# The last projection result in two column halves, and one store for four batches

## Chip, core and metric

The kernel runs on one NeuronCore of one Trainium2 chip. The metric is device time in microseconds (us) of one execution of the whole program; the time given is the median of three runs.

## What is computed

Attention over 8 batches and 8 heads with 32 global and 512 local tokens of 64 dimensions per head, followed by a gated projection. Everything is float32. Cut to what matters:

```
# attention: global queries see all 544 keys; local queries see the 32 global keys
# and local keys within a distance of 32
out_g = softmax(q_g k_all^T / 8) v_all            # (8, 8, 32, 64)
out_l = softmax([q_l k_g^T | masked q_l k_l^T] / 8) v_all   # (8, 8, 512, 64)
x = concat(out_g, out_l) over tokens, heads side by side    # (8, 544, 512)

# gate: causal depthwise convolution of 5 taps along the 544 tokens, then a sigmoid
gate = sigmoid(sum_k conv_w[k] * x shifted by 4 - k)
out  = (gate * (x @ w_val)) @ w_out               # (8, 544, 512)
```

## The kernel before

The attention is done unit by unit (32 units: 8 batches by 4 pairs of heads), the projection by function `moe` once per batch for its 512 local tokens (keys 0 to 7), and at the very end once more, with key `"g"`, for the 256 global tokens of all eight batches together. Products keep float32 accuracy by splitting each operand into a high and a low part and running three matmuls for each pair of 128 x 128 weights: high x high, high x low, low x high.

Inside `moe` there are three steps. `g1(e, t)` multiplies by `w_val` and leaves block `e` of the value (128 channels by `n` tokens) in a PSUM bank. `gv`, `gh`, `gl` multiply by the gate and split the product into the tiles `gh` and `gl`. `g2(r, e)` multiplies by `w_out`: for a block `r` of 128 tokens it accumulates, over the four `e`, twelve matmuls of 128 x 512 into one bank. `ob(r)` copies the bank to an SBUF tile (`ob` for batches, `obg` for the global tokens) and `store` writes it out. For the global tokens there are two blocks, `r` = 0 and 1, each of 128 rows: four batches by 32 tokens. In the output those rows are not contiguous, as each batch has 544 rows; `store_g` writes one batch's 32 rows at a time, alternating between the DMA queues of SyncE (SP) and ScalarE (ACT).

The order of all work is written out by hand in the table `ORDER`: each engine carries out its tasks in that order, and the numbers behind `@` name PSUM banks. The class `Plan` replays the table and keeps, in `plan.at`, which bank each result has. The table ends with the global tokens:

```
g1.g.3.3 st.6.3 g2.g.0.0@4 gv.g.3 gh.g.3:DVE g2.g.0.1 ob.7.3 g2.g.0.2 gl.g.3 g2.g.0.3
g2.g.1.0@5 st.7.3 g2.g.1.1 ob.g.0 g2.g.1.2 st.g.0 g2.g.1.3 ob.g.1 st.g.1
```

`g2.g.0.*` is block 0 in bank 4, `g2.g.1.*` block 1 in bank 5, `ob.g.*` the copies and `st.g.*` the stores. The copy of block 1 is shared by two engines: ACT copies columns 0 to 255 and VectorE (DVE) columns 256 to 511 of the same bank into the same tile. After `st.g.1` nothing is left but the wait for the stores and the end of the program. Banks of the `g1.g` results (5, 1, 4, 1) are free again by then. The two tiles of tag `gv` hold the gated products until they are split.

Of the kernel before, what the change touches and what calls it, by code (L numbers as in the profile page):

```python
# [8 lines left out]
F32 = mybir.dt.float32  # L9
# [8 lines left out]
B, H, SL, SG, D = 8, 8, 512, 32, 64  # L18
DM = H * D
KW = 5  # L20
P = 128
NDT = DM // P
# [295 lines left out]
def attention_moe(ctx, tc, qk, vw, maskd, w_val, convT, w_out, out):  # L318
    nc = tc.nc
    V, A, G, T = nc.vector, nc.scalar, nc.gpsimd, nc.tensor  # L320

    cp = ctx.enter_context(tc.tile_pool(name="cp", bufs=1))
    sb = ctx.enter_context(tc.tile_pool(name="sb", bufs=2))
    ps = ctx.enter_context(tc.tile_pool(name="ps", bufs=1, space=PSUM))

    plan = Plan()
    psum = ps.tile([P, 8, SL], F32, name="psum")

    def bank(key):
        return psum[:, plan.at[key][0], :]  # L330
# [23 lines left out]
    wvh, wvl, woh, wol = (cp.tile([P, NDT, DM], F32R, name=n) for n in ("wvh", "wvl", "woh", "wol"))  # L354
# [46 lines left out]
    def copy(name, out, in_):  # L401
        eng = plan.tasks[name].eng
        if eng == "ACT":
            A.copy(out, in_)  # L404
        else:
            (V if eng == "DVE" else G).tensor_copy(out, in_)
# [3 lines left out]
    def on_pe(ins):  # L410
        last_pe[:] = [ins.ins]
# [295 lines left out]
    def moe(key, n, x0, deps_x, deps_gate, before, store):  # L707

        box = {}
        last = before  # L710

        def g1(e, t):
            xh, xl = xs_h[x0 + t], xs_l[x0 + t]
            if t == 0:
                box["pv", e] = bank(f"g1.{key}.{e}")[:, :n]
            for q, (w, x) in enumerate(((wvh, xh), (wvh, xl), (wvl, xh))):
                on_pe(T.matmul(box["pv", e], w[:, e, t * P:t * P + P], x, start=(t == 0 and q == 0),  # L717
                         stop=(t == NDT - 1 and q == 2)))

        def gv(e):  # L720
            if e == 0:
                box["gh"] = sb.tile([P, NDT, n], F32R, tag="gh", name=f"gh{key}", bufs=1)
                box["gl"] = sb.tile([P, NDT, n], F32R, tag="gl", name=f"gl{key}", bufs=1)
            box["gv", e] = sb.tile([P, n], F32, tag="gv", name=f"gv{key}_{e}")
            V.tensor_tensor(out=box["gv", e], in0=box["pv", e], in1=gates[x0 + e], op=ALU.mult)

        def gh(e):
            copy(f"gh.{key}.{e}", box["gh"][:, e, :], box["gv", e])

        def gl(e):  # L730
            V.tensor_tensor(out=box["gl"][:, e, :], in0=box["gv", e], in1=box["gh"][:, e, :].bitcast(F32),
                            op=ALU.subtract)

        def g2(r, e):
            if e == 0:
                box["po", r] = bank(f"g2.{key}.{r}")
            rs = slice(r * P, r * P + P)
            for q, (g, w) in enumerate(((box["gh"], woh), (box["gh"], wol), (box["gl"], woh))):
                on_pe(T.matmul(box["po", r], g[:, e, rs], w[:, e, :], start=(e == 0 and q == 0),  # L739
                         stop=(e == NDT - 1 and q == 2)))  # L740

        def ob(r):
            box["ob", r] = sb.tile([P, DM], F32, tag="ob", name=f"ob{key}_{r}")
            if (key, r) == ("g", n // P - 1):
                A.copy(box["ob", r][:, :DM // 2], box["po", r][:, :DM // 2])
                V.tensor_copy(box["ob", r][:, DM // 2:], box["po", r][:, DM // 2:])
            else:
                copy(f"ob.{key}.{r}", box["ob", r], box["po", r])

        part = 693 if n == 512 else 356  # L750
        early = [f"pc{u}.{KW - 1}" for u in range(NPC)] if key == 0 else []
        for e in range(NDT):
            for t in range(NDT):
                name = f"g1.{key}.{e}.{t}"
                plan.add(name, "PE", part, lambda e=e, t=t: g1(e, t), [last, f"w{e}"] + deps_x(t) + early,
                         take=[("bank", name[:-2])] if t == 0 else [],
                         give=[("xh", x0 + t), ("xl", x0 + t)] if e == NDT - 1 else [])
                last = name
            plan.add(f"gv.{key}.{e}", "DVE", 601 if n == 512 else 334, lambda e=e: gv(e),
                     [last] + deps_gate(e) + ([f"gv.{key}.{e - 1}"] if e else []),  # L760
                     take=[("gv", f"{key}.{e}")] + ([("g", key)] if e == 0 else []),
                     give=[("bank", f"g1.{key}.{e}"), ("gate", x0 + e)])
            plan.add(f"gh.{key}.{e}", (("ACT", 520 if n == 512 else 385), ("DVE", 335 if n == 512 else 205)), 0, lambda e=e: gh(e),
                     [f"gv.{key}.{e}"], lock=True)
            plan.add(f"gl.{key}.{e}", "DVE", 600 if n == 512 else 338, lambda e=e: gl(e), [f"gh.{key}.{e}"], 
                     give=[("gv", f"{key}.{e}")], lock=True)
        for r in range(n // P):
            for e in range(NDT):
                name = f"g2.{key}.{r}.{e}"
                plan.add(name, "PE", 682, lambda r=r, e=e: g2(r, e),  # L770
                         [last, f"gl.{key}.{e}", f"w{NDT + e}"], take=[("bank", name[:-2])] if e == 0 else [],
                         give=[("g", key)] if (r, e) == (n // P - 1, NDT - 1) else [])
                last = name
            plan.add(f"ob.{key}.{r}", *(("ACT", 350) if (key, r) == ("g", n // P - 1) else ((("ACT", 470), ("DVE", 600)), 0)), lambda r=r: ob(r), [last], take=[("ob", name[3:-2])],
                     give=[("bank", name[:-2])])
            plan.add(f"st.{key}.{r}", "ACT", 800 if key == "g" else 400, lambda r=r: store(r, box["ob", r]), [f"ob.{key}.{r}"])
            plan.add(f"sd.{key}.{r}", "DMA", 620, lambda: None, [f"st.{key}.{r}"], give=[("ob", f"{key}.{r}")])
        return last
# [60 lines left out]
    for b in range(B):  # L839
# [4 lines left out]
        for h in range(2):  # L844
            n = f"{b}.{h}"
# [65 lines left out]
    for b in range(B):  # L911
        units = range(4 * b, 4 * b + 4)
        for u in units:
            plan.add(f"sig{u}", "ACT", 530, lambda u=u: sigmoid(gates[u]),
                     [f"fix{v}" if v < NHF else f"conv{v}.{KW - 2}" for v in units] + ([f"sig{u - 1}"] if u % 4 else []))
        last = moe(b, SL, 4 * b, lambda t, b=b: [f"xl{4 * b + t}"], lambda e, b=b: [f"sig{4 * b + e}"], last,
                   lambda r, o, b=b: A.dma_start(out[b, SG + r * P:SG + r * P + P, :], o))
# [16 lines left out]
    plan.add("sigg", "ACT", 1250, lambda: [sigmoid(gates[NU + dt]) for dt in range(NDT)],  # L934
             [f"gconv{dt}" for dt in range(NDT)])

    def store_g(r, o):
        for s in range(P // SG):
            (A if s % 2 else nc.sync).dma_start(out[r * (P // SG) + s, 0:SG, :], o[s * SG:s * SG + SG, :])

    moe("g", B * SG, NU, lambda t: [f"gxl{t}"], lambda e: ["sigg"], last, store_g)

    with tc.manual_schedule():
# [91 lines left out]
```

## Time and profile before

| what | value |
|---|---|
| runs | 362.12 us median of 3 (360.65 to 363.55) |
| profiled execution | 361.64 us |
| its span, first to last instruction | 359.9 us |
| mean granted TensorE clock | 0.994 of full speed |
| busy share of the span: TensorE, its weight loads, VectorE, ScalarE | 97%, 78%, 88%, 71% |
| DMA | 66.73 MB, mean 185 GB/s; 8.91 MB written |
| last matmul starts | 355.33 us |

PE is TensorE's matmul row and PEld its weight loads; an issue of a DMA is listed on the queue of the engine that issues it (SPq, ACTq), and what it moves is seen apart, as packets and as the landing. Times in the trace count from the start of the span.

### The profile page before, as it was taken

To read this page: it belongs to the slowest core of one execution; us is meant where nothing else is said; L and a number is where in the kernel's file an instruction comes from. 1 tells how busy PE (TensorE), PEld (TensorE's weight loads), DVE (VectorE), ACT (ScalarE), POOL (GpSimd) and SP (SyncE) were. 2 spreads that over 40 slices of the span, in tenths; PEclk is the share of its full clock that TensorE was granted. 3 is DMA by queue.
4 is the path that set the end of the run, shared out by engine and by line. 5 is a ranking of instruction groups with operands and counts; after the bars stand their busy time and mean duration, and the time that the engine had idled before them with its cause. 6 is when DMAs were issued, how large, how long until landed. Compare 5 with 4: busy or idle time off the path is not lost.

```text
span 359.9 us, 14810 instructions
## 1 busy us (share of the span) xinstructions
PE 349.9 (97%) x6331; PEld 280.0 (78%) x6331; DVE 315.3 (88%) x1085; ACT 254.3 (71%) x652; POOL 0.8 (0%) x7
## 2 busy tenths in 40 slices
PE   8899999899999999999999999999999999999995
PEld 4666687778787888788878877888878888888894
DVE  4899999999989899899899997989599696988981
ACT  3899999897897688987788566776659458523131
POOL 0000000000000000000000000000000000000000
PEclk9899999999999999999999999999999999999999
DMA  7995947695675734925666482823854101000223
GB/s 280 400 362 166 359 156 279 209 402 193 226 235 199 276 104 108 391 102 171 221 241 237 159 277 104 262 67 132 283 165 173 62 2 51 13 29 36 112 87 87
DMA packets 17249, 66.73 MB, mean 185 GB/s; under 512 B 1952, under 2 KB 4000, under 8 KB 17184
## 3 DMA queue, kind: packets, MB, share of 16 engines
q1 hardware_dynamic: 12240, 57.12, 45.2%
q10 hardware_dynamic: 4944, 8.67, 6.6%
q8 instruction: 49, 0.80, 0.9%
q14 instruction: 16, 0.13, 0.1%
HBM read 56.87 MB, written 8.91 MB: 183 GB/s over the span
## 4 chain that ended last, share of the span: by engine, by line
PE 81%; ACT 8%; DMA 5%; DVE 3%; issue 1%; SPq 1%; ACTq 0%; DVEq 0%
PE psum L717 25%; PE psum L739 23%; PE psum L603 7%; PE psum L567 7%; PE psum L592 7%; PE psum L632 4%; DMA v<-in_vw_dram 3%; PE psum L531 3%; DMA out_dram<-ob 2%; ACT pm L586 2%; PE psum L493 2%; ACT xs L624 2%; PE psum L511 1%; DVE gate L668 1%; ACT xc L404 1%
## 5 line engine op out<-in xcount | busy, mean ns | idle before, releaser
L586 ACT ACTIVATE pm<-pm,mx 128x128 f32<-128x128 f32 x256 | 80.9, 407 | 25.8 <-DVE mx L579 22.5
L668 DVE SCALAR_TENSOR_TENSOR gate<-xc,cw,gate 128x512 f32<-128x512 f32 x120 | 87.7, 745 | 1.1 <-ACT gate L397 0.4
L579 DVE CUSTOM_DVE_ANT_0 pm<-psum,mask 128x128 f32<-128x128 f32 x256 | 57.4, 285 | 5.2 <-PE psum L567 5.2
L717 PE MATMUL psum<-xh,wvh 128*128 128x512 f32 x128 | 53.8, 421 | 0.0
L739 PE MATMUL psum<-woh,gh 128*128 128x512 f32 x128 | 53.0, 414 | 0.0
L717 PE MATMUL psum<-xl,wvh 128*128 128x512 f32 x128 | 50.6, 396 | 0.0
L717 PE MATMUL psum<-xh,wvl 128*128 128x512 f32 x128 | 50.5, 395 | 0.0
L739 PE MATMUL psum<-woh,gl 128*128 128x512 f32 x128 | 50.2, 392 | 0.0
L739 PE MATMUL psum<-wol,gh 128*128 128x512 f32 x128 | 50.0, 391 | 0.0
L404 ACT COPY pts<-psum 128x512 f32<-128x512 f32 x49 | 28.6, 601 | 16.0 <-PE psum L592 16.0
L592 PE MATMUL psum<-ident,pm 128*128 128x128 f32 x256 | 38.0, 278 | 0.6 <-ACT pm L586 0.3
L567 PE MATMUL psum<-qk 64*32 64x128 f32 x2048 | 38.1, 281 | 0.5 <-ACT pm L586 0.4
L603 PEld LDWEIGHTS psum<-v,pts 128*32 128x32 f32 x2048 | 31.1, 111 | 8.3 <-issue 4.7
L567 PEld LDWEIGHTS psum<-qk 64*32 64x32 f32 x2048 | 30.3, 108 | 8.5 <-issue 3.6
L592 PEld LDWEIGHTS psum<-ident,pm 128*128 128x128 f32 x256 | 29.6, 140 | 9.1 <-ACT pm L586 2.7
L603 PE MATMUL psum<-v,pts 128*32 128x65 f32 x2048 | 34.9, 224 | 1.4 <-DMA v<-in_vw_dram 1.2
L717 PEld LDWEIGHTS psum<-xh,wvl 128*128 128x128 f32 x128 | 24.0, 188 | 5.6 <-issue 0.2
L739 PEld LDWEIGHTS psum<-woh,gl 128*128 128x128 f32 x128 | 24.0, 188 | 5.3
L717 PEld LDWEIGHTS psum<-xh,wvh 128*128 128x128 f32 x128 | 24.3, 190 | 4.5 <-DVE xl L664 0.2
L717 PEld LDWEIGHTS psum<-xl,wvh 128*128 128x128 f32 x128 | 24.2, 189 | 4.1 <-issue 0.2
L739 PEld LDWEIGHTS psum<-woh,gh 128*128 128x128 f32 x128 | 24.2, 189 | 4.0 <-issue 0.2
L739 PEld LDWEIGHTS psum<-wol,gh 128*128 128x128 f32 x128 | 24.2, 189 | 3.9
(111 smaller groups left out, 554.0 us busy)
## 6 DMA issues: line engine op xcount, KB each, us to landing
v<-in_vw_dram SPq DMA_DIRECT2D x32, 975.0 KB, 6.7
qk<-in_qk_dram SPq DMA_DIRECT2D x32, 624.0 KB, 5.0
out_dram<-ob ACTq DMA_DIRECT2D x32, 256.0 KB, 2.2
wraw<-in_w_val_dram SPq DMA_DIRECT2D x4, 512.0 KB, 12.3
wraw<-in_w_out_dram SPq DMA_DIRECT2D x4, 512.0 KB, 4.1
mask<-in_mask_dram SPq DMA_DIRECT2D x1, 256.0 KB, 4.6
out_dram<-obg SPq DMA_DIRECT2D x4, 64.0 KB, 1.7
out_dram<-obg ACTq DMA_DIRECT2D x4, 64.0 KB, 2.0
```

Source lines behind the costliest of these rows:

```text
L404: A.copy(out, in_)
L493: on_pe(T.matmul(s[h][SG * c:SG * c + SG, cols], qkt[rows, SL + SG * h:SL + SG * h + SG], keys, start=True, stop=True))
L531: on_pe(T.matmul(ag[SG * c:SG * c + SG, :], pgt[:k, s, SG * c:SG * c + SG], vt[:k, w, h, :], start=(n == 0), stop=(n == len(steps) - 1)))
L567: on_pe(T.matmul((sx, sy)[h][32 * j:32 * j + 32, i, :], qkt[rows, 32 * m:32 * m + 32], qkt[rows, k0:k0 + P], start=True, stop=True))
L579: V.tensor_tensor_reduce(out=pm[:, h, i, :], in0=s[:, i, :], in1=mask[:, i, :], op0=ALU.add, op1=ALU.min, scale=-SCALE, scalar=3.0e38, acc ...
L586: A.activation(out=pm[:, h, i, :], in_=pm[:, h, i, :], func=AF.Exp, bias=mx[:, c:c + 1], scale=-1.0)
L592: on_pe(T.transpose(pt[:, i, :], pm[:, h, i, :], ident))
L603: on_pe(T.matmul(ax[32 * j:32 * j + 32, h, E1 * i:E1 * i + E1], pts[:, h, i, 32 * j:32 * j + 32], vt[:, block_win(4 * i + j), h, :], start ...
L632: on_pe(T.transpose(xt[:, P * i:P * i + P], xs[:, i].rearrange("p h d -> p (h d)"), ident))
L668: V.scalar_tensor_tensor(out=acc, in0=xc[:, k:k + SL], scalar=cw[:, u % NDT, k:k + 1], in1=acc, op0=ALU.mult, op1=ALU.add)
L717: on_pe(T.matmul(box["pv", e], w[:, e, t * P:t * P + P], x, start=(t == 0 and q == 0), stop=(t == NDT - 1 and q == 2)))
L739: on_pe(T.matmul(box["po", r], g[:, e, rs], w[:, e, :], start=(e == 0 and q == 0), stop=(e == NDT - 1 and q == 2)))
```

## The change

For block 1 of the global tokens, `g2` no longer runs twelve matmuls of 512 columns. `g2_halves` first runs twelve of 256 columns for output columns 0 to 255 into bank 5 (that of `g2.g.1`), then twelve for columns 256 to 511 into another bank, that of the first `g1.g` result which neither block uses (bank 1). As soon as the first twelve are recorded, VectorE's copy of that half into a tile of its own (`obg_first`, tag `gv`) and its store on the SP queue are recorded too. `ob` copies the second half on ACT into a tile of half the width, and its store follows on the SP queue. `store_g` now writes all four batches of a block with one DMA, whose DRAM side is 4 batches by 32 rows by the columns: block 0 on the ACT queue, both halves of block 1 on the SP queue.

```diff
+        def g2_halves(r, e):
+            if e % (NDT // 2) == 0:
+                used = [plan.at[f"g2.{key}.{i}"][0] for i in (r - 1, r)]
+                spare = next(n for n in (f"g1.{key}.{i}" for i in range(NDT)) if plan.at[n][0] not in used)
+                box["half", e * 2 // NDT] = bank(spare if e else f"g2.{key}.{r}")
+            c, rs = e * 2 // NDT, slice(r * P, r * P + P)
+            for k in range(e * 2 % NDT, e * 2 % NDT + 2):
+                for q, (g, w) in enumerate(((box["gh"], woh), (box["gh"], wol), (box["gl"], woh))):
+                    on_pe(T.matmul(box["half", c][:, :DM // 2], g[:, k, rs], w[:, k, c * DM // 2:(c + 1) * DM // 2],
+                             start=(k == 0 and q == 0), stop=(k == NDT - 1 and q == 2)))
+            if (c, k) == (0, NDT - 1):
+                o = sb.tile([P, DM // 2], F32, tag="gv", name="obg_first")
+                V.tensor_copy(o, box["half", 0][:, :DM // 2])
+                store(r, o, 0)
+
         def g2(r, e):
+            if (key, r) == ("g", n // P - 1):
+                g2_halves(r, e)
+                return
...
         def ob(r):
-            box["ob", r] = sb.tile([P, DM], F32, tag="ob", name=f"ob{key}_{r}")
-            if (key, r) == ("g", n // P - 1):
-                A.copy(box["ob", r][:, :DM // 2], box["po", r][:, :DM // 2])
-                V.tensor_copy(box["ob", r][:, DM // 2:], box["po", r][:, DM // 2:])
+            last_part = (key, r) == ("g", n // P - 1)
+            o = box["ob", r] = sb.tile([P, DM // 2 if last_part else DM], F32, tag="ob", name=f"ob{key}_{r}")
+            if last_part:
+                A.copy(o, box["half", 1][:, :DM // 2])
             else:
-                copy(f"ob.{key}.{r}", box["ob", r], box["po", r])
+                copy(f"ob.{key}.{r}", o, box["po", r])
...
-    def store_g(r, o):
-        for s in range(P // SG):
-            (A if s % 2 else nc.sync).dma_start(out[r * (P // SG) + s, 0:SG, :], o[s * SG:s * SG + SG, :])
+    def store_g(r, o, c=1):
+        k = P // SG
+        cols = slice(0, DM) if r == 0 else slice(c * DM // 2, (c + 1) * DM // 2)
+        (nc.sync if r else A).dma_start(out[r * k:r * k + k, 0:SG, cols], o)
```

On the ACT queue, at the end of the program, the copies of batch results (`ob`) and their stores stay as they were, and the two blocks of global tokens (`obg`) follow. Before:

```order
L404 COPY ob_3_5936<-psum 128x512 [waits DMAHW7_49,PE_49]
L917 DMA out_dram<-ob_3_5936 128x512 [waits Activation_49]
L404 COPY obg_5952<-psum 128x512 [waits DMAHW0_49,PE_49]
L939 DMA out_dram<-obg_5952 32x512 [waits Activation_49]
L939 DMA out_dram<-obg_5952 32x512
L745 COPY obg_5964<-psum 128x256 [waits DMAHW1_49,PE_49]
L939 DMA out_dram<-obg_5964 32x512 [waits DVE_49]
L939 DMA out_dram<-obg_5964 32x512
```

And with the change:

```order
L404 COPY ob_3_5936<-psum 128x512 [waits DMAHW7_49,PE_49]
L935 DMA out_dram<-ob_3_5936 128x512 [waits Activation_49]
L404 COPY obg_5961<-psum 128x512 [waits DMAHW0_49,PE_49]
L958 DMA out_dram<-obg_5961 4x32x512 [waits Activation_49]
L764 COPY obg_5976<-psum 128x256 [waits DMAHW1_49,PE_49]
```

Two stores of block 0 have become one with three counts, and behind the last copy ACT issues nothing.

On the SP queue, which up to there issues the loads of the attention (`v`, `qk`), the end differs like this:

```order
 L416 DMA v_4954<-in_vw_dram 128x1950
 L416 DMA v_5000<-in_vw_dram 128x1950
-L939 DMA out_dram<-obg_5952 32x512 x2
-L939 DMA out_dram<-obg_5964 32x512 x2
-L1030 UNCONDITIONAL_BRANCH
+L958 DMA out_dram<-obg_first 4x32x256
+L958 DMA out_dram<-obg_5976 4x32x256
+L1049 UNCONDITIONAL_BRANCH
```

The four stores of one batch each, two for either block, have become two stores of four batches, one for either half of block 1.

## The prediction

> **What bounds the kernel now.** I read the page's head and its chain first, then the chain of work that ended last from 340 us on.
>
> ```profile
> span 359.9 us, 14810 instructions
> ...
> PE 349.9 (97%) x6331; PEld 280.0 (78%) x6331; DVE 315.3 (88%) x1085; ACT 254.3 (71%) x652; POOL 0.8 (0%) x7
> ...
> PE 81%; ACT 8%; DMA 5%; DVE 3%; issue 1%; SPq 1%; ACTq 0%; DVEq 0%
> ```
>
> ```profile
> 350.27 5.46 PE psum L739 x24
> 355.73 0.02 issue
> 355.75 0.38 ACT obg L745
> 356.13 0.02 issue
> 356.16 0.42 DVE obg L746
> ```
>
> The kernel is a TensorE kernel, 97% busy and 81% of the chain. The change touches nothing before the last 24 matmuls, so the stage that decides is the tail. There the chain is serial: the matmuls end, ACT copies the left half of the last result (0.38 us), VectorE copies the right half only after ACT (its row starts when ACT's has ended: both read one bank and write one tile), and then four stores go out. From the last copy's end at 356.58 to the end of the span at 359.9 are 3.3 us, 1% of the span, in which no compute engine works. That is nearly all the change can win, and the stores are all it can lose on.
>
> How the stores run today is seen in ACT's timeline, in the answers for the two lines that store, in SyncE's waits, and in the DMA picture of the last 3.5 us.
>
> ```profile
> 353.04 0.59 ACT L404 COPY obg<-psum 128x512 f32<-128x512 f32 x1 [2.77 <-PE psum L739]
> 353.65 0.86 ACTq L939 DMA_DIRECT2D out_dram<-obg  x2
> 355.75 0.37 ACT L745 COPY obg<-psum 128x256 f32<-128x256 f32 x1 [2.13 <-PE psum L739]
> 356.62 0.85 ACTq L939 DMA_DIRECT2D out_dram<-obg  x2
> ```
>
> ```profile
> L939 SPq DMA_DIRECT2D out_dram<-obg x4: 315/384/414, 353.6 to 357.0; - x4
> L939 ACTq DMA_DIRECT2D out_dram<-obg x4: 375/412/445, 353.7 to 357.0; - x4
> ...
> DMA to landing us min/median/max: 1.6/1.9/2.0
> ```
>
> ```profile
> L917 ACTq DMA_DIRECT2D out_dram<-ob x32: 338/338/444, 78.2 to 350.3; - x32
> ...
> DMA to landing us min/median/max: 2.0/2.2/8.2
> ```
>
> ```profile
> SPq L1030 <- DMA out_dram<-obg: 1.4, 2, 1.2
> ```
>
> ```profile
> DMA  0000000000769299949999410000000000000000
> ...
> DMA packets 192, 0.26 MB, mean 75 GB/s; under 512 B 64, under 2 KB 64, under 8 KB 192
> ```
>
> Each queue issues two stores of 64 KB, the second at 357.0, and it lands up to 2.0 us later, at 359.0; SyncE waits for it (1.2 us) and closes the program 0.9 us after that. The DMA picture covers 356.5 to 360 in 40 slices of 0.0875 us. It goes quiet after slice 24, at 358.6, so from the last packet to the span's end are 1.3 us. Of the 192 packets 64 are under 512 B, and 128 are rows of 2 KB: four stores, 16 small closing packets each. So a store of 32 rows is now cut over all 16 engines, two rows to an engine.
>
> **The change part by part.**
>
> *The matmuls.* Rows of matmuls of both widths, first and last of their runs:
>
> ```profile
> 344.42 0.28 PE L717 MATMUL psum<-xgh,wvh 128*128 128x256 f32 x1
> ...
> 349.99 0.28 PE L717 MATMUL psum<-xgh,wvl 128*128 128x256 f32 x1
> ...
> 352.83 0.39 PE L739 MATMUL psum<-woh,ghg 128*128 128x512 f32 x1
> ...
> 355.33 0.39 PE L739 MATMUL psum<-woh,glg 128*128 128x512 f32 x1
> ```
>
> The 48 matmuls of 256 columns start 5.57 / 47 = 0.1185 us apart, the last 12 of 512 columns 2.50 / 11 = 0.227 us. The change turns those 12 into 24 of 256 columns. The last one then starts at 352.83 + 23 x 0.1185 = 355.56 and ends 0.28 later, at 355.84, where today's ends at 355.72: +0.12 us. The weights are loaded 24 times in place of 12; the 256-column run pays the same load per matmul and keeps its 0.1185, so that is in the price.
>
> *The copies.* The left half is complete after 12 matmuls, at 352.83 + 11 x 0.1185 + 0.28 = 354.41. VectorE copies it (0.42 us, beside the second half's matmuls in another bank), to 354.86. Behind that copy nothing is queued on VectorE; today it idles there. The right half is copied by ACT from 355.87 to 356.24. The 0.42 us copy leaves the path: the last store can be issued at 356.28, where today the first two go out at 356.62 and the last two at 357.0. Up to here the change gains 0.34 us on the first issue and 0.74 us on the last.
>
> *The stores.* Eight issues become three: one of 256 KB on ACT at 353.65 (row block 0), and on SyncE one of 128 KB at 354.90 (left half) and one of 128 KB at 356.28 (right half). Behind them stands only SyncE's closing wait. Issue time: today's rows of this line are 0.32 to 0.45 us, and the trace has no issue of a store whose DRAM side has three counts (4 batches, 32 rows, columns). The longest single issue nearby in kind is one load's
>
> ```profile
> 2.60 0.86 SPq L416 DMA_DIRECT2D qk<-in_qk_dram  x1
> ```
>
> so the new form costs between 0 and 0.5 us more. I take 0, the nearest row (same queue, same destination), and keep 0.5 for the range.
>
> *How many engines carry a store* is the term that decides, and no row shows it. Every transfer of the trace has an outermost count of 32 or 128 and spreads over 16 engines; the new ones have 4 on the DRAM side. If the rows are still dealt out to 16 engines, an engine gets 8 of them; if the outermost count is what is dealt out, four engines get one batch of 32 rows each and the other twelve nothing. The four stores of before were each one batch: 16 engines were reached because a batch was cut by its 32 rows. I take the second: in the rows so far the cut is along the outermost count and never along an inner one. The Trainium skill has this as a rule ("DMA: Bandwidth & Descriptors", section "Why a DMA increments its semaphore by 16 and not by 1"): a copy runs on the largest number of engines up to 16 that divides the slowest count, other than 1, of both sides, which for 128 partitions and 4 batches is 4; by it the sum is the four-engine one below, without it the 16-engine one. The 16 closing packets per 32-row store agree with it, and no run here shows a count under 16.
>
> Prices for four engines, from three DMA pictures (345 to 352.5 us, 0 to 20 us, 353.5 to 356.6 us):
>
> ```profile
> DMA packets 576, 1.05 MB, mean 140 GB/s; under 512 B 64, under 2 KB 64, under 8 KB 576
> ...
> q10 hardware_dynamic: 576, 1.05, 37.6%
> ```
>
> ```profile
> DMA packets 2788, 6.93 MB, mean 347 GB/s; under 512 B 303, under 2 KB 1825, under 8 KB 2786
> ...
> q1 hardware_dynamic: 2642, 6.88, 91.0%
> ```
>
> ```profile
> DMA  0000000000000979597938989923000000000000
> ```
>
> In the first, 512 rows of 2 KB took 0.376 x 16 x 7.5 = 45.1 us of engine time: 0.088 us a row, 23.3 KB per us and engine. In the second more than half of the packets are of 1 KB (1825 less 303), and the rate is 6.88 MB / (0.91 x 16 x 20) = 23.6 KB per us: the price goes by bytes, so a row of 1 KB takes 0.044 us, with 0.088 as the far end. The third (slices of 0.0775 us) starts at 354.51: data follows the issue at 353.65 by 0.86 us.
>
> On four engines, each has to move 32 x 2 KB and twice 32 x 1 KB: 32 x 0.088 + 64 x 0.044 = 5.63 us, one store behind the other on the same four. The 256 KB store begins at 354.51 and would be done at 357.3; the left half is there from 354.90 + 0.86 = 355.8 and the right half from 357.1, so the engines never run dry, and it no longer matters when the copies end. The last packet ends at 354.51 + 5.63 = 360.14, where today's ends at 358.6: **+1.5 us**. The 1.3 us behind it stay. The copies' gain of 0.74 us and the matmuls' 0.12 us vanish in the wait for these engines.
>
> **The sum.** The profiled execution took 361.64 us, 1.7 us around its span of 359.9; 361.64 + 1.5 = **363.2 us**. (It lies 0.5 us under the median of the three runs, 362.12, and the runs span 360.65 to 363.55, so the forecast is a slight loss that a measurement of this kernel can hardly tell: about 1%, 3.6 us, is what it tells.)
>
> **The rivals.**
>
> - *Sixteen engines.* Then the 256 KB store is gone long before the others start, and the right half is one store alone, issued at 356.28. Its 128 KB lie between the 64 KB that landed in 1.6 and the 256 KB that land in 2.0 us: 1.8, landing at 358.1 against 359.0 today. With 0.5 us more for the issue the gain falls to 0.4. I take 0.9: 360.7 us. For it: DMAs are cut somewhere by rows, and the SBUF side still has 128. Against it: no row with an inner cut. This is the other side, and it decides if more than about six engines share the stores (5.63 x 4/6 = 3.75, ending at 358.3, no later than today's 358.6).
> - *Rows of 1 KB cost as much as rows of 2 KB* on four engines, and the issue is slow: 64 x 0.044 + 0.5 = 3.3 us more, 366.5 us, slower by over 1%. It needs a 1 KB row above 0.076 us; the byte rate of the 0 to 20 us picture speaks against it.
> - *The one store is issued as four again.* Four issues of 0.38 us on SyncE, the last at 357.42, landing 1.6 to 2.0 us later at 359.2 on the mean: 0.2 us later than today, 361.8 us. The three single instructions in each queue's order speak against it.
>
> **How the numbers follow.** Four engines 0.60; sixteen 0.28; taken apart 0.06; dear small rows 0.06. Single runs of before lie up to 1.5 us from their median; I take 1.2 us of scatter for a median of three. The likeliest's own range is then 362.0 to 364.9 (with the slow issue's 0.5 above). For 8 in 10 the range must also reach to the sixteen-engine case, 360.7, and take in a part of its scatter: 360.2 to 364.9. Over 1% either way needs 3.6 us: faster only by scatter on the sixteen-engine case, 0.02; slower with the dear rows or scatter on the forecast, 0.05; within it 0.93.
>
> **What would show it.** In the profile after: 24 rows of about 0.28 us and 0.1185 us apart at the new matmul line, the last ending near 355.8; VectorE's copy near 354.4 with no wait for ACT; one ACT copy as the last compute near 355.9; a SyncE issue near 356.3. With four engines the DMA picture from 354.5 on stands at two to three tenths without a gap until about 360, the three stores bring 12 small packets in place of 48, and landings of the last two stores take 3 us and more. With sixteen, short bursts near full, quiet by 357.6. The forecast is wrong if the plateau is absent, or if the span's end no longer hangs on these stores.

## The result, and the profile after

| | before | after |
|---|---|---|
| median (lowest to highest) | 361.81 us (360.65 to 363.55), 6 runs | 366.59 us (364.34 to 367.24), 6 runs |
| ratio | | 1.0109, 95% interval 1.0076 to 1.0141 |
| profiled execution, its span | 361.64, 359.9 us | 367.24, 365.3 us |

The change makes the kernel slower by about 1.1% (2.7 to 5.1 us by the interval). The forecast was 363.2 us with a range up to 364.9: the right sign, and too small.

The end of the chain of waits of the kernel after (start, length, what):

```profile
351.93 2.73 PE psum L757 x12
354.65 2.88 PE psum L742 x24
357.54 0.02 issue
357.56 0.37 ACT obg L764
```

Beside the chain of before: row block 0 of the global tokens began at 350.27 and begins at 351.93 now, and one copy stands behind the matmuls where there were two. From that point the span went on for 359.9 - 350.27 = 9.6 us, and now goes on for 365.3 - 351.93 = 13.4 us. So the tail, the only part that was changed, is longer by 3.7 us. (These pieces of the chain begin 0.16 us after block 0's first matmul does, which is at 350.11 and 351.77.) The other 1.7 us of the two spans' difference of 5.4 arose earlier, where both kernels do the same. One place is seen in TensorE's waits from 221 to 227 us, first after, then before (what waited for what, us, times, longest):

```profile
PE psum L632 <- ACT ob L404: 2.2, 1, 2.2
```

```profile
PE psum L632 <- ACT ob L404: 0.5, 1, 0.5
```

In the traces of kernels with the same work ahead of it, here and in the experiments below, block 0's first matmul starts anywhere between 350.1 and 353.4 us (the latest is e11). I take these 1.7 us for scatter, and count every tail below from that first matmul, in each kernel's own trace. The ratio agrees with that: its 1.09% is 3.9 us, about what the tail alone makes.

The tail by engine, after. ACT's timeline, VectorE's and SyncE's queue:

```profile
354.69 0.59 ACT L404 COPY obg<-psum 128x512 f32<-128x512 f32 x1 [2.77 <-PE psum L757]
355.31 1.14 ACTq L958 DMA_DIRECT2D out_dram<-obg  x1
357.56 0.37 ACT L764 COPY obg<-psum 128x256 f32<-128x256 f32 x1 [2.28 <-PE psum L742]
```

```profile
356.13 0.42 DVE L746 COPY obg_first<-psum 128x256 f32<-128x256 f32 x1 [2.95 <-PE psum L742]
```

```profile
356.58 0.69 SPq L958 DMA_DIRECT2D out_dram<-obg_first  x1
357.96 0.54 SPq L958 DMA_DIRECT2D out_dram<-obg  x1
```

All compute is done at 357.93, and the program ends 7.4 us later; before, these were 3.3 us. SyncE's waits at the end, and the DMA picture of 354 to 366 us (40 slices of 0.3 us):

```profile
SPq L1049 <- DMA out_dram<-obg_first: 4.5, 1, 4.5
SPq L1049 <- DMA out_dram<-obg: 1.3, 1, 1.3
```

```profile
DMA  2000000004150021222222222222222110000000
...
DMA packets 397, 0.54 MB, mean 45 GB/s; under 512 B 12, under 2 KB 268, under 8 KB 396
```

All rows here are those of the three new stores: the last batch store had ended by 353.7, and the 2 of slice 0 is one packet of instructions. The first row of block 0 moves at 356.6, 1.3 us after its issue, and slices 9 to 11 (counted from 0) hold 12 of its first rows. The picture books the whole time of a row in the slice in which the row starts; these rows take long, so the slices show a 4 and a 5, and those behind them nothing while the rows are still under way. From slice 15 on the stores run at two tenths of 16 engines, with 12 packets under 512 B: four closing packets for each store, where each store had 16 before. Four engines carry them, twelve are idle. Four stretches of the same picture (three of 1 us, one of 2 us):

356.6 to 357.6 us, the first rows of the 256 KB store:

```profile
DMA  2500930300039990009000000000000009900900
...
DMA packets 15, 0.03 MB, mean 31 GB/s; under 512 B 0, under 2 KB 0, under 8 KB 15
```

357.6 to 358.6 us, the next rows of that store:

```profile
DMA packets 14, 0.03 MB, mean 29 GB/s; under 512 B 0, under 2 KB 0, under 8 KB 14
```

359.3 to 360.3 us, later rows of the same store:

```profile
DMA packets 45, 0.09 MB, mean 92 GB/s; under 512 B 0, under 2 KB 0, under 8 KB 45
...
q10 hardware_dynamic: 45, 0.09, 25.4%
```

361.5 to 363.5 us, rows of 1 KB of the two halves:

```profile
DMA packets 186, 0.18 MB, mean 92 GB/s; under 512 B 6, under 2 KB 186, under 8 KB 186
```

In the steady part the four engines are full (25.4% of 16 engines is 4.06 engines): a row of 2 KB takes 4 / 45 = 0.089 us of one engine, and a row of 1 KB 2 x 4 / 180 = 0.044 us (186 packets less 6 closing ones). In the first two microseconds they move 15 and 14 rows in place of 45 each. Single rows of the first have records of up to 0.96 us.

### The profile page after: what moved, and what is told of

Same layout as the page of the kernel before. It is cut to its first block, busy times and chain, and to the rows that moved or that the text cites. A ratio compares the mean times of both kernels' runs of the same rounds, so it can differ in the third digit from the quotient of the medians.

```text
span 365.3 us, 14827 instructions
## 1 busy us (share of the span) xinstructions
PE 348.3 (95%) x6343; PEld 279.4 (76%) x6343; DVE 315.3 (86%) x1085; ACT 254.5 (70%) x652; POOL 0.9 (0%) x7
## 3 DMA queue, kind: packets, MB, share of 16 engines
HBM read 56.87 MB, written 8.91 MB: 180 GB/s over the span
## 4 chain that ended last, share of the span: by engine, by line
PE 83%; ACT 9%; DMA 3%; DVE 1%; issue 1%; ACTq 0%; DVEq 0%
PE psum L717 25%; PE psum L757 23%; PE psum L603 8%; PE psum L567 7%; PE psum L592 7%; PE psum L632 4%; ACT pm L586 3%; DMA out_dram<-ob 3%; PE psum L531 3%; PE psum L493 2%; PE psum L511 2%; ACT xs L624 1%; PE psum L821 1%; ACT pts L404 1%; PE psum L742 1%
## 5 line engine op out<-in xcount | busy, mean ns | idle before, releaser
L567 PE MATMUL psum<-qk 64*32 64x128 f32 x2048 | 36.8, 273 | 1.6 <-issue 0.7
L567 PEld LDWEIGHTS psum<-qk 64*32 64x32 f32 x2048 | 29.2, 106 | 9.5 <-issue 4.2
L603 PE MATMUL psum<-v,pts 128*32 128x65 f32 x2048 | 34.1, 221 | 1.7 <-ACT diag L682 1.6
L725 DVE TENSOR_TENSOR gv<-psum,gate 128x512 f32<-128x512 f32 x32 | 21.9, 686 | 7.3 <-PE psum L717 6.8
```

The costliest lines, as they stand in the source:

```text
L567: on_pe(T.matmul((sx, sy)[h][32 * j:32 * j + 32, i, :], qkt[rows, 32 * m:32 * m + 32], qkt[rows, k0:k0 + P], start=True, stop=True))
L603: on_pe(T.matmul(ax[32 * j:32 * j + 32, h, E1 * i:E1 * i + E1], pts[:, h, i, 32 * j:32 * j + 32], vt[:, block_win(4 * i + j), h, :], start ...
```

## The experiments

The theory from these views: **the stores alone** make the loss, because four engines carry them and because these start slowly; the halves work and are not seen. Rivals: the halves cost something (24 weight loads, the other copy order); any store with three counts is slow whatever its engines; rows of 1 KB are dear; ACT's queue is a bad place for the 256 KB store.

All tails in one table, in us after the first matmul of block 0, read from each trace's instruction and packet records. The ratio is to the kernel before on the same chip; that of e7 rests on two runs. In every row the difference of the tails, as a share of the kernel, lies within the ratio's interval.

| kernel | engines | closing packets | last copy ends | last packet | span ends | ratio (95%) |
|---|---|---|---|---|---|---|
| before | 16 | 128 | 6.47 | 8.53 | 9.75 | |
| after | 4 | 12 | 6.16 | 12.23 | 13.58 | 1.0109 (1.0076 to 1.0141) |
| e1 halves, old stores | 16 | 192 | 7.70 | 9.55 | 10.96 | 1.0048 (1.0026 to 1.0071) |
| e2 new stores, no halves | 4 | 8 | 6.47 | 12.46 | 13.86 | 1.0116 (1.0081 to 1.0151) |
| e3 after, 16 engines | 16 | 48 | 6.16 | 7.91 | 9.29 | 0.9999 (0.9972 to 1.0026) |
| e4 after, block 0 old | 16, halves 4 | 72 | 6.16 | 9.60 | 10.76 | 1.0023 (0.9997 to 1.0049) |
| e5 before, block 0 new on ACT | 4, block 1 16 | 68 | 6.47 | 9.84 | 11.29 | 1.0058 (1.0016 to 1.0099) |
| e6 after, 8 engines | 8 | 24 | 6.16 | 8.78 | 10.13 | 1.0014 (0.9985 to 1.0043) |
| e7 after, 2 engines | 2 | 12 (six stores) | 6.16 | 17.52 | 18.68 | 1.0255 (1.0190 to 1.0319) |
| e8 halves, old stores reordered | 16 | 192 | 6.16 | 8.36 | 9.67 | 0.9997 (0.9967 to 1.0028) |
| e9 16 engines, no halves | 16 | 32 | 6.47 | 8.63 | 10.05 | 0.9993 (0.9962 to 1.0023) |
| e10 as e5, on SP | 4, block 1 16 | 68 | 6.47 | 9.86 | 11.31 | 1.0019 (0.9982 to 1.0057) |
| e11 before, last batch store on 4 | 16, that store 4 | 136 | 6.84 | 8.91 | 10.20 | 0.9994 (0.9962 to 1.0026) |

### One part without the other

**e1**, the halves with stores of one batch each (edit against after):

```diff
-        (nc.sync if r else A).dma_start(out[r * k:r * k + k, 0:SG, cols], o)
+        for s in range(k):
+            (A if s % 2 else nc.sync).dma_start(out[r * k + s, 0:SG, cols], o[s * SG:s * SG + SG, :])
```

> The column halves of the change, but every store covers one batch as before: 32 rows of 2 KB for block 0 and 32 rows of 1 KB for either half, alternating between the two queues (12 stores, each over 16 engines). Theory A (the loss is all in the stores that cover four batches): the copies' gain is seen, the last issue lies at about 0.7 us after the last copy's end less 0.4, the last landing some 0.5 us earlier than before, so 0.3 to 0.9 us faster than before (about 361.2 us). Theory B (the halves themselves cost: 12 more matmuls and their code, or a copy that is late): slower than before by 1 us or more, 363 us and up.

Measured: 363.85 us, 1.0048 (1.0026 to 1.0071), slower than before, though on 16 engines; the tail ends 1.2 us later than before. The cause is a fault of the experiment, seen in ACT's timeline:

```profile
355.81 0.85 ACTq L959 DMA_DIRECT2D out_dram<-obg_first  x2
356.76 0.59 ACT L404 COPY obg<-psum 128x512 f32<-128x512 f32 x1 [5.62 <-PE psum L742]
357.38 0.85 ACTq L959 DMA_DIRECT2D out_dram<-obg  x2
358.33 0.37 ACT L764 COPY obg<-psum 128x256 f32<-128x256 f32 x1 [0.97 <-ACT obg L404]
```

The stores of the left half stand in ACT's order ahead of the copy of block 0. They wait for VectorE's copy, and ACT waits with them: the copy of block 0, which came 2.92 us after block 0's first matmul in the kernel after, came at 5.77 here, and the last copy ended at 7.70 in place of 6.16. So e1 says nothing on the halves; e8 has the stores in another order.

**e2**, the stores without the halves (edit against before):

```diff
-        for s in range(P // SG):
-            (A if s % 2 else nc.sync).dma_start(out[r * (P // SG) + s, 0:SG, :], o[s * SG:s * SG + SG, :])
+        k = P // SG
+        (nc.sync if r else A).dma_start(out[r * k:r * k + k, 0:SG, :], o)
```

> The four-batch stores alone: block 1 is made and copied as before (12 matmuls, ACT then VectorE), each block is written with one store of 4 batches x 32 rows x 2 KB. Theory A: four engines carry 128 KB each, the tail is as long as in the changed kernel, about 3.8 us longer than before from block 0's copy to the end: about 365.5 us. Theory B: close to before, within 1 us of 361.8.

Measured: 365.63 us, 1.0116 (1.0081 to 1.0151), the same loss as after, with matmuls, copies and tiles of before. All rows are 2 KB here, so dear small rows are out, and so are the halves as a cause. Its DMA picture, 354.1 to 366 us:

```profile
DMA  0002413022222222223122222111000000000000
...
DMA packets 264, 0.52 MB, mean 44 GB/s; under 512 B 8, under 2 KB 8, under 8 KB 264
```

Two stores, eight closing packets, two tenths: four engines again, and a thin start.

**e8**, the halves with old stores in an order in which no store waits ahead of a copy (edit against after):

```diff
-        (nc.sync if r else A).dma_start(out[r * k:r * k + k, 0:SG, cols], o)
+        for s in range(k):
+            eng = A if r == 0 or (c == 1 and s % 2) else nc.sync
+            eng.dma_start(out[r * k + s, 0:SG, cols], o[s * SG:s * SG + SG, :])
```

> The halves with stores of one batch again, now with the four stores of the left half all on SyncE's queue and those of block 0 all on ACT's, so that no copy of ACT stands behind a store that waits for VectorE (in the first try with one-batch stores block 0's copy came 2.8 us late for that reason). Theory A: the last copy ends 0.3 us earlier than before, the end of the program 0.3 to 0.5 us earlier in the tail, total 361.5 us, not to be told from before. Theory B (the halves cost by themselves): tail longer than before's 9.75 us, total above 363 us.

Measured: 362.75 us, 0.9997 (0.9967 to 1.0028). The last copy ends 0.31 us earlier than before and the span 0.08 us: twelve issues have taken most of it back. The halves do no harm, and what they gain is too small to be measured.

**e4**, only block 0 as before, the halves in the new form (edit against after):

```diff
+        if r == 0:
+            for s in range(k):
+                (A if s % 2 else nc.sync).dma_start(out[s, 0:SG, :], o[s * SG:s * SG + SG, :])
+        else:
+            nc.sync.dma_start(out[r * k:r * k + k, 0:SG, c * DM // 2:(c + 1) * DM // 2], o)
```

> The changed kernel with block 0 stored batch by batch as before; only the two half stores cover four batches. Four engines then carry 64 KB each (2.7 us) in place of 128 KB. If the slow first rows of 1.5 us came with the 256 KB store on ACT's queue and are gone: the right half's store alone decides, issued at 356.3 on before's clock, last packet near 358.6: no change, 361.5 to 362. If each first store of this form pays them: last packet near 360.1, about 363.3 us.

Measured: 363.09 us, 1.0023 (0.9997 to 1.0049). The tail ends 1.0 us later than before and 2.8 us earlier than after. In SyncE's order the left half's store stands ahead of two of block 0's stores and holds them up, so this is an upper bound for what the halves' stores cost alone. Without block 0's store in the new form 2.8 of the 3.8 us are gone; that store alone makes 1.5 (e5, below). The two parts cost more together than each by itself: in the kernel after, the halves' rows come behind block 0's on the same four engines.

The left half's store also shows a start of its own, on engines that were idle: its first row moves at 357.4, 1.3 us after the issue, and 61 rows of 1 KB follow in the first microsecond, where 90 is the steady number. No record of them is above 0.21 us.

### The number of engines

**e3** and **e9**. The rows of the global tokens are laid out token by token instead of batch by batch (`gv` writes its columns in that order, so the partition is token x 4 + batch), and the DRAM side of a store becomes 32 tokens by 4 batches by columns: the same three counts, bytes and row lengths, with 32 outermost. e3 has the halves, e9 has block 1 as before.

```diff
-            V.tensor_tensor(out=box["gv", e], in0=box["pv", e], in1=gates[x0 + e], op=ALU.mult)
+            if key == "g":
+                o = box["gv", e].rearrange("p (r q b) -> p r b q", r=2, q=SG)
+                i0, i1 = (x.rearrange("p (r b q) -> p r b q", r=2, q=SG) for x in (box["pv", e], gates[x0 + e]))
+                V.tensor_tensor(out=o, in0=i0, in1=i1, op=ALU.mult)
...
-        (nc.sync if r else A).dma_start(out[r * k:r * k + k, 0:SG, cols], o)
+        (nc.sync if r else A).dma_start(out[r * k:r * k + k, 0:SG, cols].rearrange("b q c -> q b c"), o)
```

> The changed kernel, still with three stores of three counts, but with the tokens of a block ordered token by batch (the gated product is written in that order), so that the DRAM side of a store is 32 tokens x 4 batches x columns, its outermost count 32 in place of 4. Theory A1 (the number of engines follows the outermost count): 48 closing packets in place of 12, the DMA picture in short bursts near full, last packet before 359 in the time of before's span: about 361.0 us, as e1 or a little better. Theory A2 (a store with three counts is itself slow, in its issue of 0.5 to 1.1 us and its first rows of 0.2 to 0.9 us, whatever the engines): 16 engines but 1 to 2 us of slow first rows, 362.5 to 364 us. If the cut still goes by batches: as the changed kernel, 366 us.

Measured: 361.94 us, 0.9999 (0.9972 to 1.0026): the loss is gone. The picture of 352 to 360 us (slices of 0.2 us), and the microsecond from 353.0, in which its 256 KB store begins (0.025 us):

```profile
DMA  0000079970049500019800000000000000000000
...
DMA packets 432, 0.52 MB, mean 66 GB/s; under 512 B 48, under 2 KB 304, under 8 KB 432
```

```profile
DMA  0492796898699289689948948994852200000000
...
DMA packets 144, 0.26 MB, mean 262 GB/s; under 512 B 16, under 2 KB 16, under 8 KB 144
```

Three bursts near full, 3 x 16 closing packets. All 128 rows of block 0 are through in 0.8 us, with no slow start, where after moved 15 rows in its first microsecond. So a store with three counts is not slow by itself. Its issue is longer than that of a one-batch store, though; the rows of the storing line in e3 (duration ns min/median/max, start us):

```profile
L963 ACTq DMA_DIRECT2D out_dram<-obg x1: 667/667/667, 351.7 to 351.7; - x1
L963 SPq DMA_DIRECT2D out_dram<-obg_first x1: 652/652/652, 353.0 to 353.0; - x1
L963 SPq DMA_DIRECT2D out_dram<-obg x1: 539/539/539, 354.4 to 354.4; - x1
```

The tail ends at 9.29 against before's 9.75. That is the gain which the change had to give, 0.46 us or 0.13% of the kernel, under what the ratio's interval (0.3% either way) can show; what the other order of `gv`'s writes costs ahead of the tail is in the ratio and not separated.

> Block 1 made and copied as before (12 matmuls of 512 columns, ACT then VectorE), stores of four batches on sixteen engines by the token-by-batch order: two stores in place of eight. Theory A: the store form is neutral once it has sixteen engines; the tail is 9.6 us, between before's 9.75 and the 9.3 of the version with halves and sixteen engines; total 361.8 us. Theory B (most of that version's gain is from the stores): 9.3 us or less.

Measured: 362.14 us, 0.9993 (0.9962 to 1.0023). Two stores in place of eight on 16 engines, and the tail ends 0.3 us later than before: fewer stores gain nothing here.

**e6**, eight engines: a block is 16 tokens of all eight batches, so that the outermost count is 8 (edit against after, with `gv` laid out to match, as in e3).

```diff
-        (nc.sync if r else A).dma_start(out[r * k:r * k + k, 0:SG, cols], o)
+        (nc.sync if r else A).dma_start(out[:, r * (SG // 2):(r + 1) * (SG // 2), cols], o)
```

> The changed kernel with the tokens of the global part dealt to the two blocks differently: a block holds 16 tokens of all eight batches, so the DRAM side of a store is 8 batches x 16 tokens x columns, outermost count 8. If the number of engines follows the outermost count: 24 closing packets, a plateau at half of the share of sixteen, 64 KB per engine in all (2.7 us). With the slow first rows of about 1.5 us that the four-engine store showed: last packet about 9.1 us after the first matmul of block 0 (before 8.5, changed kernel 12.2), 362.5 us. Without them 8.1 us, 361.5 us. If the engines do not follow the count: as with sixteen, 7.9 us.

Measured: 363.06 us, 1.0014 (0.9985 to 1.0043). From 354.5 to 363 us (slices of 0.21 us), then the first microsecond of the 256 KB store:

```profile
DMA  0000166525155455555554100000000000000000
...
DMA packets 408, 0.52 MB, mean 62 GB/s; under 512 B 24, under 2 KB 280, under 8 KB 408
```

```profile
DMA packets 27, 0.06 MB, mean 55 GB/s; under 512 B 0, under 2 KB 0, under 8 KB 27
```

24 closing packets for three stores, a plateau of five tenths, and the slow start again: 27 rows in the first microsecond, where eight engines move 90 at the steady 0.089 us.

**e7**, two engines: each store cut in two by batches (edit against after).

```diff
-        (nc.sync if r else A).dma_start(out[r * k:r * k + k, 0:SG, cols], o)
+        for s in range(0, k, 2):
+            (nc.sync if r else A).dma_start(out[r * k + s:r * k + s + 2, 0:SG, cols], o[s * SG:(s + 2) * SG, :])
```

> The changed kernel with every store cut in two by batches: 2 batches x 32 rows x columns, outermost count 2, six stores. If the number of engines follows the outermost count: 2 x 6 = 12 closing packets, a plateau at one eighth, 256 KB on each of two engines (10.7 us at 24 KB per us): last packet about 17 us after the first matmul of block 0, about 370.5 us. If the loss were that of the three-count form or of the number of issues and not of the engines: at or below the changed kernel's 366.6 us.

Measured: 372.18 us, 1.0255 (1.0190 to 1.0319), from two runs. From 355.2 to 372 us (slices of 0.42 us):

```profile
DMA  0001101111111110111111111111111000000000
...
DMA packets 396, 0.52 MB, mean 31 GB/s; under 512 B 12, under 2 KB 268, under 8 KB 396
```

One tenth for 12 us, six stores with two closing packets each. From the issue at 3.54 to the last packet are 13.98 us: 1.3 to the first row and 12.7 of rows, where twice the steady rows of four engines (32 x 0.089 + 64 x 0.044 = 5.7 us) would be 11.4. SyncE's four issues take 0.67, 0.93, 1.53 and 2.62 us one after the other, while the two engines still work off earlier rows; what stretches them is not shown.

### The slow start

**e5** and **e10**, before with block 0 alone as one store of four batches, on ACT's queue in e5 and on SP's in e10 (edit of e5; e10 has `nc.sync` for `A`).

```diff
     def store_g(r, o):
+        if r == 0:
+            A.dma_start(out[0:P // SG, 0:SG, :], o)
+            return
```

> Before, with only block 0 stored by one store of four batches, on ACT's queue; block 1 as before (one bank, ACT then VectorE, four stores of one batch). Nothing else is on the DMA engines when block 0's store starts, so its first rows are seen alone. If a four-engine store pays about 2 us at its start by itself: first 16 rows in 1.5 us, its last packet about 9.3 us after the first matmul of block 0 (4.84 + 2.0 + 32 x 0.080), with block 1's rows on the same engines the end about 1.7 us later than before. If the slow rows came only from the collision with SyncE's store: last packet at 7.4, and the end as before.

> The same with block 0's store on SyncE's queue. If the slow start is ACT's (its sequencer busy 1.1 us with the issue): gone here. If it belongs to the store's form on four engines: the same 1.5 us, and an issue of 0.7 to 1.1 us on SyncE.

Measured: 363.67 us, 1.0058 (1.0016 to 1.0099), and 363.16 us, 1.0019 (0.9982 to 1.0057); the tails end at 11.29 and 11.31. SP issues the store in 0.71 us and ACT in 1.14, and the end is the same. The first microsecond of the store in e10:

```profile
DMA packets 15, 0.03 MB, mean 31 GB/s; under 512 B 0, under 2 KB 0, under 8 KB 15
```

15 rows, as in e5 and in the kernel after. Neither the queue nor the length of the issue makes the slow start.

**e11**, four engines with a store of two counts: in before, the last batch's last store (128 rows) is cut into 124 and 4 rows, both multiples of 4 and not of 8.

```diff
+    def store_l(r, o, b):
+        for lo, hi in (((0, 124), (124, P)) if (b, r) == (B - 1, P // SG - 1) else ((0, P),)):
+            A.dma_start(out[b, SG + r * P + lo:SG + r * P + hi, :], o[lo:hi, :])
...
```

> Before, with the last store of a batch's results (128 rows of 2 KB, one run of rows, on ACT's queue) cut into one of 124 rows and one of 4. 124 is not divisible by 8 or 16, so if the number of engines is a divisor of the outermost count both run on four engines, 31 rows and 1 row each. Issue of the two-count form 0.34 to 0.44 us, first rows 0.85 us after the issue. If slow first rows belong to four engines: the first 16 rows take 1.5 us here too, the store 4.5 us in all. If they belong to the three-count form: 31 x 0.084 = 2.6 us from the first row to the last, no slow rows. If the cut is not by divisors: 16 or more engines' closing packets and 0.7 us. The total stays within 0.5 us of before in each case, since only a store beside the last matmuls is longer.

Measured: 362.47 us, 0.9994 (0.9962 to 1.0026). The store of 124 rows runs on four engines. The two microseconds from 354.3, in which it starts:

```profile
DMA packets 19, 0.04 MB, mean 39 GB/s; under 512 B 0, under 2 KB 0, under 8 KB 19
```

```profile
DMA packets 23, 0.05 MB, mean 47 GB/s; under 512 B 0, under 2 KB 0, under 8 KB 23
```

The slow start is there without a third count, if a little weaker: 42 rows in the two microseconds, where after has 29. The first row comes 0.79 us after this store's issue, near the 0.86 of the two-count store from which the prediction took it, and not 1.3. The total shows nothing, since this store has 10 us until the program ends. The tail does: it ends 0.45 us later than before, because ACT's copy of block 1 came 0.4 us late: it waited for this store, which still read the tile.

```profile
359.38 0.37 ACT L745 COPY obg<-psum 128x256 f32<-128x256 f32 x1 [2.51 <-DMA out_dram<-ob]
```

## Why the prediction was right or wrong

- **The stage, and what bounds it.** Right: the tail alone, and in it the stores. The halves and the copies came as worked out: the last matmul ends 5.76 us after block 0's first, against 5.73 forecast; ACT's copy starts at 5.79, forecast 5.76, and the last store is issued at 6.19, forecast 6.17. They are worth nothing in the kernel after because the engines are busy until 12.2.
- **How many engines carry a store.** Right, and shown by more than one count: outermost counts of 2, 4, 8, 32 and 124 ran on 2, 4, 8, 16 and 4 engines. The Trainium skill has it so ("DMA: Bandwidth & Descriptors", section "Why a DMA increments its semaphore by 16 and not by 1": the largest number up to 16 that divides the slowest count of both sides), and these five counts agree.
- **What four engines cost.** Here the prediction failed. Its term was 0.86 us to the first data and 32 x 0.088 + 64 x 0.044 = 5.63 us of rows, 6.5 us from the issue to the last packet and +1.5 us at the end. The issue came as forecast, at 3.54 us in the tail's time, and the last packet at 12.23: 8.7 us. The steady price was right: with 0.089 and 0.044 us the rows make 5.7 us. Two things were missing. The first row came 1.3 us after the issue, 0.44 more than the 0.86 that the prediction took; e3 and e9, with three counts on 16 engines, have the same 1.3, and e11, with two counts on four, has 0.79. And the time from first to last row is 7.4 us, 1.8 more than the forecast's 5.63 and 1.7 more than the steady rows make. Most of that is the engines' slow start: 29 rows in the first two microseconds in place of 90 lose 1.4 us. 0.44 + 1.8 + 1.5 = 3.7 us, and the tail is longer by 3.7 to 3.8.
- **The issue** was bounded by 0 to 0.5 us more. After has 1.14 on ACT, 0.69 and 0.54 on SP, so on ACT even the bound was too low. It moved nothing by itself (e5 and e10 end together); what mattered was the delay of the first row, for which the prediction took the rows of another form of store. Its 0.86 us was also the first row on SyncE's queue; in the same trace ACT's store, issued in the same moment, has its first row 1.15 us after the issue, and 0.84 where ACT issues alone (e8).
- **The rival of dear 1 KB rows** was wrong, and came near the measured time by chance: 1 KB rows cost half of 2 KB rows, and e2, without any, is as slow. **Sixteen engines** was not what happened, but e3 makes it happen: its tail is 0.46 us shorter than before's, where the rival had 0.9 and, with the long issue, 0.4. The stores were not issued as four again.
- **The range** let the unknown form of store cost 0.5 us at most, in one of its three parts (issue, first data, rows). It had no row for the other two and took the nearest ones as exact.

Why a store on few engines starts slowly stays open. With rows of 2 KB and engines that were idle before, it does so on 2, 4 and 8 engines, from either queue, with two counts or three; in e3 and e9, on 16, all 128 rows are through in 0.8 us. Few engines alone don't make it. In e2 block 1's store, of the same form, arrives while block 0's last rows are on the same four engines, and in the first microsecond from its first row they move 29 of its rows and 18 of block 0's, the full rate; the halves' rows that follow block 0's in the kernel after show no such start either. And in e4 a store of 1 KB rows on four idle engines starts far less slowly. Its size alone is not the reason, since e7's first store, of the same 128 KB but with rows of 2 KB on two engines, moves 11 rows in its first microsecond in place of 22. The shorter rows may be it, or the shorter pause: the engines had been idle for 0.8 us there, for 0.2 us in e11 (42 rows in two microseconds) and for 3.0 us in after (29 rows). No run separates these.

No version beat the kernel before measurably: e3, e8 and e9 lie at 0.9999, 0.9997 and 0.9993, each with an interval that holds 1. The part of the end that the change could have won was 0.5 us.

## What to carry to other kernels

Look at the outermost count of a store before joining several into one: joined by batches it went from 16 engines to 4 and cost 1.1 to 1.2%, joined with the tokens outermost it cost nothing that can be measured, and even so joining eight stores into two gained nothing that can be measured. A store in a compute engine's queue that waits for another engine's data holds up every copy behind it (2.85 us in e1), so it goes behind them or on another queue. And a transfer form that the trace has never shown gets a range for each of its parts: issue, first data, first rows, steady rows.

## What the runs showed that I had not expected

- Stores of 2 KB rows on fewer than 16 engines that were idle before start slowly: with four engines 15 rows in the first microsecond and single rows of up to 0.96 us, against 45 rows per microsecond later. With eight engines 27 rows in the first microsecond.
- A store with three counts takes longer to issue. The first in its queue took 0.65 to 0.75 us on SP; on ACT it took 0.66 to 0.67 with 16 engines and 1.13 to 1.20 with fewer. With two counts it was 0.32 to 0.47 on 16 engines and 0.51 on four (e11). The first row of a store with three counts comes 1.3 us after the issue, on 4 as on 16 engines; with two counts 0.8 to 0.9, and 1.0 to 1.15 for ACT's store where SP issues one in the same moment.
